# Packed attention with a gated convolution: the same instructions in another written-out order

## The chip, the cores and the metric

The kernel runs on one core of a Trainium2 chip. The metric is the device time of one execution in microseconds (us). Three runs of the kernel before took 290.02, 289.56 and 290.32 us; their median is 290.02 us.

## What is computed

For each of 8 batches, 8 heads of width 64 attend in two stages: 32 learned queries `p` attend to the 576 keys and values, and the 576 queries `q` attend to the 32 packed results. The heads side by side are `x` (576 x 512 a batch), which goes through a causal convolution over 5 positions, a sigmoid gate, a product with `w_val` and a product with `w_out`:

```python
p_packed = sm_attn(p, k, v)             # 32 x 64 per head
x        = sm_attn(q, p_packed, p_packed)
gate_pre += conv_w[k] * xp[:, k:k + S]  # k = 0..4, causal
out      = (sigmoid(gate_pre) * (x @ w_val)) @ w_out
```

`w_val`, `conv_w` and `w_out` reach the kernel as 64-bit floats, so each weight comes as two 32-bit words, and the kernel itself makes two float32 parts of them.

## The kernel before, in words

The work of one batch is cut into **streams**, Python generators that issue a few instructions and yield. The table `streams` (line 656) names them by a letter, and the text `ORDER` (line 50) says which stream takes its next step when: `W0.3` is three steps of stream W, `a2` one step of batch 2's stream a. Instructions stand in the queues of the engines in exactly that order (`InOrder`, line 76, ties each to the one before it on its engine). Nothing is rearranged later, so the text is the schedule, and an instruction whose input is late holds up all that stands behind it on its engine.

Capital letters load or prepare weights. `L` loads the word tiles of `w_val` (wv0 to wv3, 512 KB each), of `conv_w` and of `w_out` (wo0 to wo3). `P`, `K`, `Q`, `V` load p (two batches at once, four transfers of 64 KB) and k, q, v of a batch (two transfers of 576 KB each). All are issued by SyncE (SP) in one queue. `W` turns wv0 to wv3 into the float32 tile `wv`: a tile takes two ScalarE instructions (`top`, `words`), three on VectorE and two on GpSimd (`from_double`, line 232, and line 257). `O` does the same for `w_out` and splits it into a high and a low part, `woh` and `wol`; `C` does it for `conv_w`, turns it on TensorE (`cwps`, `spread`) and leaves `cwb`.

Small letters are the work of a batch:

- `k`, `q`: VectorE transposes p, k, q (`pT`, `kT`, `qT`).
- `a` (`attn_pack`, line 349): scores `s1` on TensorE, their row maximum `nb1` on VectorE, exp on ScalarE (`a1`), a turn on TensorE (`at`), its copy `a1t` on ScalarE, the product with v (`pv`), the scaled copy `ppd`.
- `p`: the turn of `ppd` (`ppTt`) and its copy `ppT`.
- `s`, `t`: scores `s2`, and their softmax by VectorE, GpSimd and ScalarE in `t2`; the result is `a2` with a high part `a2h` and a low part `a2l`.
- `w`: packed values times `wv` (`wp`), split into `wph` and `wpl`.
- `x` (`mixed`): the attention output. In batches 0 to 2 TensorE does the convolution as well (`convolved`, line 508: 80 small matmuls a half, with `kx` = `ppd` times `cwb`); from batch 3 on stream `g` does it on VectorE, 16 instructions a batch.
- `v` (`value`, line 571): 12 long matmuls for each quarter of the columns (`val`), the gated product `sig`, its high part `gvh` (ScalarE) and low part `gvl` (GpSimd).
- `o` (`project`, line 617): the product with `w_out`, 12 long matmuls for each chunk of 128 output rows, its copy `osb`, and the store. Even batches do chunks 0 to 3 of their pair, odd batches 4 to 8. A chunk accumulates in the one PSUM buffer of tag `out` (`PSB`, line 44), so the next chunk's first matmul waits for the `osb` of the chunk before it. For the last batch (line 621) chunks 4 to 8 are accumulated together, three of four column quarters ahead of the last one; there chunk 4 and 5 share one buffer, and chunk 7 has the `out` buffer.

The profiler names an instruction by its tiles without numbers: `s`, `pv`, `x`, `val`, `o` are these matmuls, and all have line 84, that of the helper.

## Time and profile before

| What | Value |
|---|---|
| median of three runs | 290.02 us |
| the profiled execution, its own time | 290.36 us |
| its span in the trace | 288.6 us |
| first matmul | 12.92 us |
| first matmul of `val` (batch 0) | 59.2 us |
| busy: TensorE, VectorE, ScalarE, GpSimd | 257.3, 236.6, 163.7, 127.8 us |
| read from and written to HBM | 33.57 MB, 9.44 MB |

Times inside the trace count from the start of the span; the execution's own time is 1.76 us more than the span. A busy TensorE is not a TensorE at its peak: matmuls overlap, and one that runs at half the clock counts as busy all the same.

### The profile page before, as it was taken

How to read it: one execution, taken by the hardware profiler on the slowest of the kernel's cores; microseconds unless marked ns; L12 is line 12 of the kernel's file. 1: busy time of each engine (PE TensorE's matmuls, PEld its weight loads, DVE VectorE, ACT ScalarE, POOL GpSimd, SP SyncE). 2: the span in 40 equal slices, each digit the busy share in tenths (PEclk: the TensorE clock that was granted, in tenths of full speed). 3: DMA queues.
4: the chain of work that ended last, by engine and by line, in shares of the span. 5: the costliest groups of instructions: out<-in, count | busy, mean ns of one | idle time of the engine just before them, and what ended most of it. 6: DMA issues, size and time to landing. Idle time of an engine off the chain costs nothing.

```text
span 288.6 us, 8496 instructions
## 1 busy us (share of the span) xinstructions
PE 257.3 (89%) x3676; PEld 190.6 (66%) x3676; DVE 236.6 (82%) x313; ACT 163.7 (57%) x306; POOL 127.8 (44%) x118
## 2 busy tenths in 40 slices
PE   0147758998999999999999999999999999999994
PEld 0025446476677867678678778676887688688873
DVE  0599478598989897869999999999999899777811
ACT  2363464457873646666583776566684763754322
POOL 0153668736798972305335631534044534312410
PEclk9999999999999999999999999999999999999999
DMA  6999962649576849451136456421411111111104
GB/s 238 337 354 314 297 228 75 218 131 301 185 216 201 274 111 271 154 156 41 40 125 209 140 194 204 125 75 39 118 39 39 74 39 73 40 73 73 39 0 182
DMA packets 25839, 43.56 MB, mean 151 GB/s; under 512 B 5829, under 2 KB 11973, under 8 KB 25802
## 3 DMA queue, kind: packets, MB, share of 16 engines
q1 hardware_dynamic: 25802, 43.02, 46.3%
q8 instruction: 29, 0.48, 0.7%
q14 instruction: 8, 0.07, 0.1%
HBM read 33.57 MB, written 9.44 MB: 149 GB/s over the span
## 4 chain that ended last, share of the span: by engine, by line
PE 65%; DVE 22%; ACT 5%; DMA 4%; issue 2%; POOL 0%; SPq 0%; ACTq 0%; DVEq 0%
PE o L84 27%; PE val L84 13%; DVE sig L84 10%; PE s L84 7%; PE x L84 7%; PE pv L84 4%; DMA wv_words<-in_moe_w_val_dram 4%; PE wp L84 2%; PE at L84 2%; DVE qT L84 2%; DVE t L84 2%; DVE mx L84 2%; DVE kT L84 1%; ACT sig L84 1%; DVE rs L84 1%
## 5 line engine op out<-in xcount | busy, mean ns | idle before, releaser
L84 POOL TENSOR_TENSOR gvl<-sig,gvh 128x576 fp32r<-128x576 f32 x32 | 49.0, 1533 | 85.5 <-ACT gvh L84 85.5
L84 DVE SCALAR_TENSOR_TENSOR sig<-xp,cw,sig 128x576 f32<-128x576 f32 x80 | 73.4, 917 | 6.1 <-ACT sig L84 4.5
L84 PE MATMUL o<-woh,gvh 128*128 128x512 f32 x144 | 58.6, 407 | 0.7 <-ACT osb L84 0.7
L84 PE MATMUL o<-woh,gvl 128*128 128x512 f32 x144 | 56.8, 395 | 0.0
L84 PE MATMUL o<-wol,gvh 128*128 128x512 f32 x144 | 56.7, 394 | 0.0
L84 PE MATMUL val<-a2h,wph 128*128 128x288 f32 x128 | 39.3, 307 | 0.1
L84 PE MATMUL val<-a2h,wpl 128*128 128x288 f32 x128 | 37.8, 295 | 0.0
L84 PE MATMUL val<-a2l,wph 128*128 128x288 f32 x128 | 37.7, 295 | 0.0
L84 PEld LDWEIGHTS o<-woh,gvh 128*128 128x128 f32 x144 | 27.0, 188 | 11.3 <-ACT osb L84 2.1
L84 ACT ACTIVATE osb<-o 128x512 f32<-128x512 f32 x34 | 20.2, 596 | 22.1 <-PE o L84 18.0
L84 PEld LDWEIGHTS o<-woh,gvl 128*128 128x128 f32 x144 | 27.0, 188 | 6.4
L84 ACT CAST gvh<-sig 128x576 fp32r<-128x576 f32 x32 | 21.5, 671 | 16.6 <-DVE sig L84 16.4
L84 PEld LDWEIGHTS o<-wol,gvh 128*128 128x128 f32 x144 | 27.1, 188 | 5.0
L84 PE MATMUL s<-kT,pT 32*32 32x288 f32 x512 | 17.2, 480 | 14.2 <-DVE kT L84 13.3
L84 DVE SCALAR_TENSOR_TENSOR sig<-sig,val 128x576 f32<-128x576 f32 x32 | 23.7, 740 | 7.5 <-PE val L84 4.5
L84 PEld LDWEIGHTS val<-a2h,wph 128*128 128x128 f32 x128 | 24.0, 188 | 5.7 <-issue 1.3
L84 POOL TENSOR_TENSOR t<-t,rs 128x576 f32<-128x576 f32 x16 | 20.8, 1298 | 14.7 <-DVE rs L84 14.5
L84 PEld LDWEIGHTS val<-a2h,wpl 128*128 128x128 f32 x128 | 24.1, 188 | 0.6
L84 PEld LDWEIGHTS val<-a2l,wph 128*128 128x128 f32 x128 | 24.1, 188 | 0.0
L84 PE MATMUL pv<-vm,a1t 96*32 96x64 f32 x768 | 17.0, 244 | 7.9 <-ACT a1t L84 7.3
L84 PEld LDWEIGHTS pv<-vm,a1t 96*32 96x32 f32 x768 | 13.8, 125 | 15.3 <-ACT a1t L84 9.7
L84 POOL TENSOR_TENSOR t<-t,mx 128x576 f32<-128x576 f32 x16 | 18.5, 1159 | 11.0 <-DVE mx L84 9.9
(80 smaller groups left out, 452.0 us busy)
## 6 DMA issues: line engine op xcount, KB each, us to landing
km<-in_k_dram SPq DMA_DIRECT2D x16, 576.0 KB, 5.9
vm<-in_v_dram SPq DMA_DIRECT2D x16, 576.0 KB, 5.8
qm<-in_q_dram SPq DMA_DIRECT2D x16, 576.0 KB, 6.0
out_dram<-osb SPq DMA_DIRECT2D x36, 256.0 KB, 2.0
wv_words<-in_moe_w_val_dram SPq DMA_DIRECT2D x4, 512.0 KB, 4.4
wo_words<-in_moe_w_out_dram SPq DMA_DIRECT2D x4, 512.0 KB, 5.8
p<-in_p_dram SPq DMA_DIRECT2D x16, 64.0 KB, 5.5
cw_words<-in_moe_conv_w_dram SPq DMA_DIRECT2D x1, 20.0 KB
```

Source lines behind the costliest of these rows:

```text
L84: made = getattr(self.engine, op)(*args, **kw)
```

## The change

Only the text of `ORDER` changes. Every stream takes the same number of steps, so every engine executes the same instructions on the same data; what changes is where they stand. The first line and the last lines of the table:

```diff
-L0 W0 L0.2 P0.2 k0 K0.2 L0 W0 L0 W0.2 L0 k0 K1 W0.2 k0 V0 W0.3 a0 O0 K1 O0 W0.2 Q0 W0.2 a0.3 V0 Q0 W0 O0 k1 W0 C0.2 O0
+L0 K0 W0.3 P0 K0 W0.2 L0 P0 W0.3 k0.3 W0.4 L0 a0 K1 W0.2 V0 W0.4 L0 W0.2 K1 a0.2 W0 a0.3 W0 a0 L0 k1 a0 C0.2 W0 k1
...
-v7 g7 v7 g7 v7 o7.2 g7 v7 o6 o7.2 v7.2 o7.15
+o6 g7 v7.2 g7 o6 g7.2 o6 g7.2 v7 o6 x7 g7.2 v7 g7.2 v7.4 g7 o6.2 g7.3 v7.2 g7.4 v7.3 o7 g7 o7.2 v7.3 o7.2 o6 o7.14
+o6.3
```

**SyncE, start of the program, before** (`wv` are tiles of w_val, `km` halves of k, `vm` of v; the number after the name is the batch, or for `wv` and `wo` the tile):

```order
L84 DMA wv0_words_77<-in_moe_w_val_dram 128x1024
L84 DMA wv1_words_81<-in_moe_w_val_dram 128x1024
L84 DMA wv2_words_83<-in_moe_w_val_dram 128x1024
L84 DMA p_0_85<-in_p_dram 32x8x64 x4
L84 DMA km_0_0_93<-in_k_dram 128x2x576
L84 DMA km_0_1_95<-in_k_dram 128x2x576
L84 DMA wv3_words_97<-in_moe_w_val_dram 128x1024
L84 DMA cw_words_100<-in_moe_conv_w_dram 5x1024
L84 DMA wo0_words_104<-in_moe_w_out_dram 128x1024
L84 DMA km_1_0_108<-in_k_dram 128x2x576
L84 DMA vm_0_0_114<-in_v_dram 96x4x384
```

and in the changed kernel:

```order
L84 DMA wv0_words_77<-in_moe_w_val_dram 128x1024
L84 DMA km_0_0_79<-in_k_dram 128x2x576
L84 DMA p_0_85<-in_p_dram 32x8x64 x4
L84 DMA km_0_1_90<-in_k_dram 128x2x576
L84 DMA wv1_words_94<-in_moe_w_val_dram 128x1024
L84 DMA wv2_words_111<-in_moe_w_val_dram 128x1024
L84 DMA km_1_0_148<-in_k_dram 128x2x576
L84 DMA vm_0_0_152<-in_v_dram 96x4x384
L84 DMA wv3_words_159<-in_moe_w_val_dram 128x1024
L84 DMA km_1_1_163<-in_k_dram 128x2x576
L84 DMA cw_words_193<-in_moe_conv_w_dram 5x1024
```

k of batch 0 now stands ahead of wv1 and wv2, k of batch 1 and v of batch 0 ahead of wv3; the first tile of `w_out` has gone from the ninth entry to behind the first v and q.

**ScalarE, its row behind the first exp, before** (`a1` is the exp, `top` and `words` the two weight instructions of a tile):

```order
L84 ACTIVATE a1_0_0_168,sm1_0_120<-s1_0_0_121,nb1_0_0_166 128x576
L84 ACTIVATE wv2_top_180<-wv2_words_83 128x512
L84 ACTIVATE cw_top_182<-cw_words_100 5x512
L84 ACTIVATE cw_words_100<-cw_words_100 5x512
L84 ACTIVATE a1_0_1_186,sm1_0_120<-s1_0_1_122,nb1_0_1_170 128x576
L84 ACTIVATE wv2_words_83<-wv2_words_83 128x512
L84 COPY a1t_0_0_199<-at_0_0_200 96x768
```

and in the changed kernel:

```order
L84 ACTIVATE a1_0_0_167,sm1_0_113<-s1_0_0_114,nb1_0_0_165 128x576
L84 ACTIVATE a1_0_1_172,sm1_0_113<-s1_0_1_115,nb1_0_1_170 128x576
L84 ACTIVATE wv3_top_176<-wv3_words_159 128x512
L84 COPY a1t_0_0_179<-at_0_0_180 96x768
L84 ACTIVATE cw_top_198<-cw_words_193 5x512
L84 ACTIVATE cw_words_193<-cw_words_193 5x512
L84 ACTIVATE wv3_words_159<-wv3_words_159 128x512
```

Between the first exp and the copy `a1t` four weight instructions stood; one is left, and three have gone behind the copy. On VectorE the three instructions of wv0 now come first of all, and those of wv1 and wv2 stand between `kT` and `nb1` of batch 0.

**TensorE, the first two chunks of batch 5's projection, before** (`o_5_4` is chunk 4, `val_6_0` the first quarter of batch 6's values; the last three of 12 matmuls and the first three of the next 12):

```order
L84 MATMUL o_5_4_3321<-woh_70,gvh_643 128x512
L84 MATMUL o_5_4_3321<-wol_71,gvh_643 128x512
L84 MATMUL o_5_4_3321<-woh_70,gvl_644 128x512
L84 MATMUL val_6_0_3334<-a2h_6_2924,wph_6_3311 128x288
L84 MATMUL val_6_0_3334<-a2h_6_2924,wpl_6_3312 128x288
L84 MATMUL val_6_0_3334<-a2l_6_2925,wph_6_3311 128x288
```

and in the changed kernel:

```order
L84 MATMUL o_5_4_3312<-woh_70,gvh_461 128x512
L84 MATMUL o_5_4_3312<-wol_71,gvh_461 128x512
L84 MATMUL o_5_4_3312<-woh_70,gvl_462 128x512
L84 MATMUL o_5_5_3340<-woh_70,gvh_461 128x512
L84 MATMUL o_5_5_3340<-wol_71,gvh_461 128x512
L84 MATMUL o_5_5_3340<-woh_70,gvl_462 128x512
```

Chunk 5 now follows chunk 4 at once; the 12 matmuls of `val_6_0` that stood between them come behind both. Three other places on TensorE matter below: `wp` of batch 0 stood behind the first half of `x` and now stands ahead of it; between chunks 2 and 3 of batch 4 there stood `x`, 12 matmuls of `val` and `x`, and now one `x` alone; and the 12 matmuls of batch 6's chunk 3 stood ahead of `val_7_3` and are now the last on the engine, behind the last product of batch 7. In all else TensorE's order moves by a place or two.

## The prediction

> **What bounds the kernel now.** The first view is the page's busy line, then the busy time by stage (columns: stretch, its length, busy time and instructions of TensorE, its weight loads, VectorE, ScalarE, GpSimd; granted clock, DMA share, GB/s).

> ```profile
> PE 257.3 (89%) x3676; PEld 190.6 (66%) x3676; DVE 236.6 (82%) x313; ACT 163.7 (57%) x306; POOL 127.8 (44%) x118
> 0.00:12.90 12.90, 0.00 (x0) 0.00 (x0) 2.77 (x5) 4.25 (x6) 0.70 (x6) 1.00 0.86 299
> 12.90:59.20 46.30, 34.42 (x763) 20.83 (x763) 36.30 (x51) 22.75 (x48) 29.20 (x25) 1.00 0.77 240
> 59.20:130.00 70.80, 69.60 (x1343) 51.63 (x1341) 61.31 (x88) 45.30 (x95) 41.02 (x37) 1.00 0.66 202
> 130.00:185.00 55.00, 54.29 (x716) 41.68 (x713) 54.06 (x71) 35.80 (x63) 24.23 (x21) 1.00 0.45 141
> 185.00:281.00 96.00, 95.98 (x851) 74.33 (x849) 80.80 (x101) 53.80 (x92) 32.68 (x29) 1.00 0.15 54
> ```

> From 59.2 to 281 us TensorE is busy in 219.9 of 221.8 us: nothing reordered there can gain much unless work disappears, and none does. VectorE is as full only from 130 to 185 us (54.06 of 55). The time that can be won lies ahead of 59.2 us. How much TensorE has to do there, the chain of waits tells (start, length, what):

> ```profile
> 14.51 2.44 PE s L84 x47
> 22.73 1.51 PE pv L84 x48
> ...
> 32.08 2.57 PE s L84 x63
> ...
> 47.72 5.00 PE x L84 x80
> 52.72 1.19 PE wp L84 x16
> ...
> 59.22 1.80 PE val L84 x12
> ...
> 79.76 2.66 PE x L84 x80
> ...
> 89.52 2.78 PE o L84 x12
> ...
> 211.66 0.81 PE pv L84 x48
> ...
> 217.37 1.54 PE s L84 x63
> ...
> 269.77 11.22 PE o L84 x48
> ```

> The same 48 `pv` take 1.51 us early and 0.81 late, `s` 2.57 and 1.54, 80 `x` 5.00 and 2.66: until after 47.7 us the array runs at about half speed, though the stage rows put the granted clock at 1.00. So the first 59 us hold 12.9 us without a matmul and then small, slow matmuls between waits; from there on the program is a dense row of long matmuls (0.234 us each for `o`, 11.22/48). If that row starts earlier by some us and stays dense, the end comes earlier by as much.

> **The start, step by step.** These rows of the timeline carry it (start, length, engine, operation; in brackets the idle time before it and who ended it):

> ```profile
> 0.74 1.32 SPq L84 DMA_DIRECT2D wv_words<-in_moe_w_val_dram  x3
> ...
> 9.43 0.63 ACT L84 ACTIVATE p<-p 128x512 f32<-128x512 f32 x1 [4.78 <-DMA p<-in_p_dram]
> 10.09 0.45 DVE L84 STREAM_TRANSPOSE pT<-p 128x256 f32<-128x256 f32 x1 [10.09 <-ACT p L84]
> 12.79 0.39 DVE L84 TENSOR_SCALAR wv_words<-wv_top 128x512 uint32<-128x512 uint32 x1
> 13.09 1.37 DVE L84 STREAM_TRANSPOSE kT<-km 128x1152 f32<-128x1152 f32 x1
> 16.98 1.42 DVE L84 TENSOR_REDUCE nb<-s 128x1 f32<-128x576 f32 x2
> 17.77 0.74 ACT L84 ACTIVATE a<-s,nb 128x576 f32<-128x576 f32 x1 [1.88 <-DVE nb L84]
> 20.09 0.65 ACT L84 ACTIVATE cw_words<-cw_words 5x512 f32<-5x512 uint32 x1
> 21.90 0.77 ACT L84 COPY a1t<-at 96x768 f32<-96x768 f32 x1
> 22.73 1.51 PE L84 MATMUL pv<-vm,a1t 96*32 96x64 f32 x48 [3.08 <-ACT a1t L84]
> 34.67 0.79 DVE L84 STREAM_TRANSPOSE t<-s 128x576 f32<-128x576 f32 x1 [3.62 <-PE s L84]
> 45.57 0.78 DVE L84 STREAM_TRANSPOSE a<-t 128x576 f32<-128x576 f32 x1 [1.04 <-POOL t L84]
> 45.50 1.54 POOL L84 TENSOR_TENSOR kx<-ppd,cwb 128x640 f32<-128x640 f32 x1
> ```

> and these of the windows (last column GB/s) and of the tile `wv_words` (ns, minimum, median, maximum):

> ```profile
> 0.00:10.00 10.00, 0.00 (x0) 0.00 (x0) 0.00 (x0) 2.51 (x4) 0.70 (x6) 1.00 0.80 263
> 10.00:20.00 10.00, 4.57 (x76) 1.85 (x76) 9.77 (x13) 4.88 (x10) 4.87 (x4) 1.00 0.96 342
> L84 DVE SCALAR_TENSOR_TENSOR wv_top<-wv_top,wv_words x4: 629/1054/1674, 10.9 to 43.9; 128x512 uint32<-128x512 uint32 x4
> ```

> *Loads.* SP's first entries move 3 tiles of w_val (0.524 MB each), p (0.262) and k (1.180) before k is whole: 3.01 MB. Now it is one tile, p and k: 1.97 MB, two tiles less, worth 3.1 to 4.0 us at 342 or 263 GB/s. 1.97 MB at 263 GB/s is in by 7.5 us; p, in front of k's second half, between 5.2 and 7.5. I take 7.3, since p lands late now (9.43). Then p's scaling 0.63, `pT` 0.45, two `kT` of 1.37, hand-overs 0.2: `kT` whole at 11.3 instead of 14.46 (13.09+1.37). **3.1 us earlier**; at least 1 if the small rows of p stay the slow part.

> *To the first `pv`.* Behind `kT` VectorE now has six weight instructions ahead of `nb`: for wv1 and wv2 two of 0.39 and one SCALAR_TENSOR_TENSOR each. That one took from 0.63 to 1.67 us, the long one beside GpSimd work. With wv1 at 0.63 and wv2 at 1.67 the six end at 11.3+3.9=15.2, `nb` (2 x 0.71) at 15.9 and 16.6, the second exp at 17.6 (0.74+0.19 for its sum). On ScalarE one weight instruction (0.66) stands ahead of `a1t`: copy done at 19.0, `pv` at 19.1 against 22.73. **3.6 earlier**: the three weight instructions put behind the copy give back what the six on VectorE take. [...]

> *To the scores of q.* VectorE goes on at 17.6 with the sums (0.3), `pT`, two `kT`: 21.1. Scores of batch 1 21.2 to 23.8, `pv` 25.3; `ppd`, one exp in between, 1.5; `ppTt` 0.9, `ppT` 0.5: `s2` of batch 0 at 28.4 against 32.08. The q transposes (two of 1.37 behind `nb` at 25.4) end at 28.2, so they do not hold it. **3.6 earlier**; v and q stand in the load queue earlier than they are used.

> *To `x` and `val`.* From the end of `s2` to the last `a2` there are now 34.67 to 46.35 us, 11.7. The new chain has the same links, with `kx` and the low part of the first half ahead of the second half's product on GpSimd: about the same, `a2` whole at 31.0+11.7=42.7. Before, `x` then waited to 47.72 for `kx` (45.50+1.54) and a `ppTt`; now `kx` lies earlier, and `x` starts at 42.9, **4.8 earlier**. From `x` to `val` there were 11.5 us; `wp` (1.19) has left that stretch for the wait ahead of it, and `ppTt` (0.5, half speed) has come in, with waits of a few tenths for PSUM: 11.0, so `val` at 53.9 instead of 59.22, 5.3 earlier. A dozen hand-overs in this sum are priced at their old values; I take **5.0**, with ends at 1.5 (the loads bring 1.0 and only half a us is won later) and 6.5.

> The weights lose nothing that is needed: `wv` is whole before `wp` asks; the first `w_out` tile is late by some 15 us, but `o` first asks at 89.52 us. That slack covers it; without it each us late would be a us on the end.

> **The dense part and the end.**

> ```profile
> 280.58 0.40 PE L84 MATMUL o<-woh,gvl 128*128 128x512 f32 x1
> 281.01 0.60 ACT L84 ACTIVATE osb<-o 128x512 f32<-128x512 f32 x1 [4.25 <-PE o L84]
> 281.66 0.50 PE L84 MATMUL o<-woh,gvh 128*128 128x512 f32 x1 [0.69 <-ACT osb L84]
> 282.73 0.69 DVE L84 TENSOR_SCALAR osb<-o 128x512 f32<-128x512 f32 x1 [6.68 <-PE o L84]
> 276.90 1.43 POOL L84 TENSOR_TENSOR gvl<-sig,gvh 128x576 fp32r<-128x576 f32 x1 [4.68 <-ACT gvh L84]
> PE x L84 <- DVE a L84: 0.5, 1, 0.5
> ```

> The price of a matmul that waits for the copy of the one before it is there: 1.08 us from start to start (280.58 to 281.66) instead of 0.23, so **0.85**. Chunk 5 of batch 5 right behind chunk 4 pays all of it. Chunk 3 of batch 4 behind one `x` (some 0.7 us) pays 0.2. Together 1.05; nothing if TensorE would have waited anyway, 2.5 if ScalarE is held up ahead of these copies. In return `a2` of batch 5, for which `x` waited 0.5, now stands further ahead of it: -0.5. Other moves are two places or less and count as nothing: VectorE's order has the gated products and `a2` on average earlier against TensorE's than before.

> At the end the 12 matmuls of batch 6's chunk 3 (2.8 us) stand last. The sum of TensorE's work is the same, but two waits arise: the chunk needs chunk 7's buffer, whose copy by VectorE takes 0.69 plus 0.15 for the hand-over and is covered by chunk 8's three matmuls (3 x 0.234) only: +0.2. And the last quarter is asked for 2.8 us sooner after `val_7_2`, while its `gvl` (276.90+1.43=278.33) was ready 2.25 us ahead of the matmul that takes it (280.58): 2.8 less 2.25 is 0.5, of which ScalarE gives some back, since it no longer copies chunk 3 (0.60) in between: +0.3. Together **+0.5**; at most 2.8, if the last chain does not move at all.

> Sum against the profiled execution: -5.0 -0.5 +1.05 +0.5 = -3.95, 290.36 to 286.4. The median of the runs is 0.34 under that execution, so the median after comes to **286.1 us**.

> **Rivals.**

> *The clock comes earlier (faster).* The rows of `x` show the half speed kept through 80 matmuls from 47.72 on, 5.00 us, and gone by 79.76. If full speed is reached before `x`, that `x` takes 2.66: 2.3 us more, 283.8; with the start's upper end 282.7. For it: the work from `spread` to `pv` stands closer together now, `wp` included. Against: gaps of 0.6 to 2 us ahead of `x` remain, as before. [...]

> *The start's gain does not arrive (no change).* p may land no earlier than k's second half, and ScalarE or VectorE may be held up by wv1 and wv2, which now land later than they are queued for. With 1.5 won at the start, -1.5 -0.5 +1.05 +0.5 is -0.45: 289.6.

> *VectorE sets the end (slower).* It is busy 54.06 of 55 us from 130 to 185. If its queue, and not TensorE, sets the pace from there on, the last `gvl` stays at 278.33, and 27 matmuls come behind it instead of 15. TensorE then ends at 278.33 + 25 x 0.234 + 0.85 + 0.3 = 285.3 where it ended at 284.7, and the 1.05 of chunk waits delay VectorE's own inputs: +1.7, 291.7. It decides if VectorE cannot begin batch 3's gate sooner. Against it: VectorE has 9.5 us free between 59.2 and 130 (70.80-61.31), and that gate starts from an `x` of TensorE's row.

> **How the numbers follow.** The forecast has 0.70, the clock rival 0.10, no change 0.09, slower 0.11. The forecast's own range is 283.2 (start 6.5, waits half) to 289.0 (start at 2.1). The range for all, 282.7 to 289.6, takes in the clock rival and the edge of no change and leaves out slower and a little at each end. A measurement of this kernel tells about 0.3% (0.87 us) from no change: faster is below 289.15. Faster 0.80, same 0.09, slower 0.11.

> **What would show it.** In the changed kernel's trace: first matmul near 9.9 us, first `pv` near 19, `s2` of batch 0 near 28.4, `x` near 43, first `val` near 54, each within 1.5 us; the first `o` by about as much earlier as `val`; a wait of 0.7 of `o` for `osb` twice, in batch 5 and at the end; the last matmul near 281. It is wrong if the first `val` comes after 57.5, or if that gain is there and TensorE's row behind it has new waits of more than 2.5 us in sum.

## The result, and the profile after

| Kernel | Median | Runs | Ratio to before, 95% interval |
|---|---|---|---|
| before | 290.01 us | 8 (289.07 to 291.42) | |
| changed | 287.76 us | 8 (286.24 to 288.72) | 0.9916 (0.9888 to 0.9944) |
| changed, a second time (e9 below) | 287.10 us | 11 (285.75 to 289.43) | 0.9911 (0.9880 to 0.9943) |

The change is a gain of 2.25 us, where 3.95 was forecast. Over all 19 runs the median is 287.24, a gain of 2.8. The profiled execution shown here took 288.72 us, the longest of the first eight (span 286.9); the one profiled later took 287.10 (span 285.3). All fences of this section are of this first execution. Executions over 1.5% above the fastest of their kernel on a chip (two of e5's, one each of e8's and e12's, three of before's) are left out of the medians and ratios below.

The busy line of the page and the same five stretches as before (columns as there):

```profile
PE 257.1 (90%) x3676; PEld 191.0 (67%) x3676; DVE 236.1 (82%) x313; ACT 164.6 (57%) x306; POOL 132.3 (46%) x118
0.00:12.90 12.90, 3.56 (x64) 1.14 (x64) 6.73 (x11) 5.68 (x8) 3.66 (x9) 1.00 0.84 295
12.90:59.20 46.30, 32.82 (x802) 21.36 (x799) 37.97 (x55) 25.02 (x53) 27.42 (x25) 0.82 0.84 246
59.20:130.00 70.80, 69.92 (x1325) 52.83 (x1325) 59.01 (x80) 44.33 (x92) 41.07 (x37) 0.98 0.68 199
130.00:185.00 55.00, 55.00 (x662) 43.07 (x658) 51.98 (x71) 35.35 (x64) 24.16 (x20) 1.00 0.44 135
185.00:281.00 96.00, 93.60 (x834) 71.20 (x833) 80.40 (x99) 53.60 (x90) 36.02 (x29) 1.00 0.18 63
```

TensorE now works in the first stretch (3.56 us), and the second holds 39 matmuls more in less busy time. The 0.82 there is not a slower clock than before: the record of the granted clock begins at 53.07 us in the trace of before and at 22.12 us here, and what lies ahead of it is printed as 1.00, though 63 `s` took 2.57 us there in before, and 1.54 later. The last stretch, where TensorE was busy for 95.98 of 96 us, now has 2.4 us of gaps. One of them, 0.69 us, was there before too, but at 281.66, outside the stretch; the rest gives back a part of the gain.

The start (timeline; start, length, in brackets the idle time before and who ended it):

```profile
6.87 0.63 ACT L84 ACTIVATE p<-p 128x512 f32<-128x512 f32 x1 [1.61 <-DMA p<-in_p_dram]
7.90 2.59 DVE L84 STREAM_TRANSPOSE kT<-km 128x1152 f32<-128x1152 f32 x2
13.94 1.39 DVE L84 TENSOR_SCALAR wv_words<-wv_top 128x512 uint32<-128x512 uint32 x1
15.25 1.41 DVE L84 TENSOR_REDUCE nb<-s 128x1 f32<-128x576 f32 x2
18.87 1.51 PE L84 MATMUL pv<-vm,a1t 96*32 96x64 f32 x48 [0.97 <-ACT a1t L84]
25.69 1.07 PE L84 MATMUL pv<-vm,a1t 96*32 96x64 f32 x27 [2.03 <-issue]
29.68 2.59 PE L84 MATMUL s<-qT,ppT 32*32 32x288 f32 x64 [0.57 <-ACT ppT L84]
35.28 1.70 PE L84 MATMUL spread<-cw_top,ident 5*32 5x64 f32 x51 [1.52 <-issue]
43.59 3.47 PE L84 MATMUL x<-a,kx 32*64 32x288 f32 x80
52.86 0.40 PE L84 MATMUL val<-a2h,wph 128*128 128x288 f32 x1
57.13 0.31 PE L84 MATMUL pv<-vm,a1t 96*32 96x64 f32 x5
59.13 1.04 PE L84 MATMUL pv<-vm,a1t 96*32 96x64 f32 x43 [1.69 <-issue]
```

`kT` is whole at 10.49 (it was 14.46), the first `pv` comes at 18.87 (22.73), the first `val` at 52.86 (59.2): 6.3 us earlier. New is the word "issue": in three rows of small matmuls TensorE stops in the middle of a group that waits for no data, for 2.03, 1.52 and 1.69 us. The third costs more than its length, as the clock column of two windows shows (the third number from the end of the row):

```profile
43.60:47.00 3.40, 3.28 (x86) 1.84 (x81) 3.40 (x5) 1.96 (x5) 2.77 (x3) 1.00 0.09 21
60.10:63.20 3.10, 3.10 (x13) 2.90 (x12) 0.40 (x1) 1.15 (x3) 1.31 (x2) 0.52 0.55 134
```

and the chain of waits (start, length, what):

```profile
57.44 1.69 issue
59.13 1.04 PE pv L84 x43
60.17 3.12 PE val L84 x12
64.04 1.78 PE val L84 x12
```

`x` already runs at full granted clock (80 matmuls in 3.47 us; it was 5.00, and 2.66 in later rows), but right behind the third gap the clock is halved, and the 12 `val` from 60.17 take 3.12 us where those from 64.04 take 1.78. The rows of TensorE from 185 us on that begin with a wait, and the last copy:

```profile
227.70 0.50 PE L84 MATMUL o<-woh,gvh 128*128 128x512 f32 x1 [0.69 <-ACT osb L84]
237.20 0.51 PE L84 MATMUL o<-woh,gvh 128*128 128x512 f32 x1 [0.27 <-ACT osb L84]
264.56 0.50 PE L84 MATMUL o<-woh,gvh 128*128 128x512 f32 x1 [0.59 <-DVE sig L84]
276.97 0.50 PE L84 MATMUL o<-woh,gvh 128*128 128x512 f32 x1 [0.69 <-ACT osb L84]
283.25 0.60 ACT L84 ACTIVATE osb<-o 128x512 f32<-128x512 f32 x1 [2.58 <-PE o L84]
```

The first is chunk 5 behind chunk 4 of batch 5, as forecast; the third, at the first product of batch 7, waits for a `val` buffer that `sig` still reads, and was not forecast. The fourth is the one that stood at 281.66.

### The profile page after: what moved, and what is told of

Same layout as the page of the kernel before. It is cut to its first block, busy times and chain, and to the rows that moved or that the text cites. A ratio compares the mean times of both kernels' runs of the same rounds, so it can differ in the third digit from the quotient of the medians.

```text
span 286.9 us, 8501 instructions
## 1 busy us (share of the span) xinstructions
PE 257.1 (90%) x3676; PEld 191.0 (67%) x3676; DVE 236.1 (82%) x313; ACT 164.6 (57%) x306; POOL 132.3 (46%) x118
## 4 chain that ended last, share of the span: by engine, by line
PE 66%; DVE 18%; ACT 6%; issue 4%; DMA 2%; POOL 1%; SPq 1%; ACTq 0%; DVEq 0%
PE o L84 26%; PE val L84 13%; DVE sig L84 10%; PE s L84 8%; PE x L84 7%; PE pv L84 5%; PE at L84 4%; DMA wv_words<-in_moe_w_val_dram 2%; PE wp L84 2%; ACT sig L84 1%; PE ppTt L84 1%; ACT a L84 1%; SPq L84 1%; PE spread L84 1%; DVE a2l L84 1%
## 5 line engine op out<-in xcount | busy, mean ns | idle before, releaser
L84 POOL TENSOR_TENSOR gvl<-sig,gvh 128x576 fp32r<-128x576 f32 x32 | 51.3, 1604 | 64.7 <-ACT gvh L84 64.5
L84 DVE SCALAR_TENSOR_TENSOR sig<-xp,cw,sig 128x576 f32<-128x576 f32 x80 | 71.1, 888 | 3.2 <-ACT sig L84 1.8
L84 PE MATMUL o<-woh,gvh 128*128 128x512 f32 x144 | 58.9, 409 | 2.3 <-ACT osb L84 1.6
L84 PE MATMUL o<-woh,gvl 128*128 128x512 f32 x144 | 56.9, 395 | 0.0
L84 PE MATMUL o<-wol,gvh 128*128 128x512 f32 x144 | 56.7, 394 | 0.0
L84 PE MATMUL val<-a2h,wph 128*128 128x288 f32 x128 | 39.9, 312 | 0.0
L84 PE MATMUL val<-a2h,wpl 128*128 128x288 f32 x128 | 38.5, 301 | 0.0
L84 PE MATMUL val<-a2l,wph 128*128 128x288 f32 x128 | 38.2, 299 | 0.0
L84 PEld LDWEIGHTS o<-woh,gvh 128*128 128x128 f32 x144 | 27.0, 188 | 13.7 <-ACT osb L84 3.6
L84 ACT CAST gvh<-sig 128x576 fp32r<-128x576 f32 x32 | 21.6, 674 | 25.3 <-DVE sig L84 25.2
L84 DVE SCALAR_TENSOR_TENSOR sig<-sig,val 128x576 f32<-128x576 f32 x32 | 23.7, 740 | 10.5 <-PE val L84 7.0
L84 PEld LDWEIGHTS o<-woh,gvl 128*128 128x128 f32 x144 | 27.1, 188 | 6.8 <-POOL gvl L84 0.5
L84 ACT ACTIVATE osb<-o 128x512 f32<-128x512 f32 x34 | 20.3, 596 | 17.8 <-PE o L84 14.8
L84 PEld LDWEIGHTS o<-wol,gvh 128*128 128x128 f32 x144 | 27.1, 188 | 5.0
L84 POOL TENSOR_TENSOR t<-t,mx 128x576 f32<-128x576 f32 x16 | 20.1, 1254 | 21.8 <-DVE mx L84 21.8
L84 POOL TENSOR_TENSOR t<-t,rs 128x576 f32<-128x576 f32 x16 | 21.9, 1368 | 17.4 <-DVE rs L84 17.3
L84 PEld LDWEIGHTS val<-a2h,wph 128*128 128x128 f32 x128 | 24.6, 192 | 5.2 <-issue 2.0
L84 PEld LDWEIGHTS val<-a2h,wpl 128*128 128x128 f32 x128 | 24.6, 192 | 0.8 <-DVE wpl L84 0.3
L84 PEld LDWEIGHTS val<-a2l,wph 128*128 128x128 f32 x128 | 24.6, 192 | 0.0
L84 ACT ACTIVATE sig<-sig 128x576 f32<-128x576 f32 x20 | 13.7, 685 | 19.0 <-DVE sig L84 18.9
L84 PE MATMUL s<-kT,pT 32*32 32x288 f32 x512 | 16.0, 461 | 9.5 <-DVE kT L84 9.3
L84 PEld LDWEIGHTS pv<-vm,a1t 96*32 96x32 f32 x768 | 13.3, 119 | 13.9 <-issue 6.1
```

The source lines that it names most:

```text
L84: made = getattr(self.engine, op)(*args, **kw)
```

## The experiments

**The start and the rest apart (e1, e2, e9, e10).** e1 has the changed order up to the first `val` of batch 0, and from there the steps that are left, in the order of before. e2 is the other way round.

The seam of e1, against the changed order (what is left of each stream follows as it stands in before):

```diff
 O0.3 q1 a2 O0 x0 p1 a2.2 k3 V2 L0 v0
-v0 a2.2 K3 v0 a2 O0 K3 a2 s1 x1 a2 k3 O0 s1 a2
+K3 O0 K3 a2 v0 k3 a2.2 k3 s1 a2 s1 x1 v0 a2 s1
...
```

Expected of e1: 

> The changed order up to the first val of batch 0, from there on the order of before. Theory (the gain is made ahead of the first val; a part is lost again by a gap of TensorE inside pv of batch 2, where it waits for no data, by the half clock behind it, and later by the chunk waits of batch 5 and by VectorE): the first val starts near 53 us as in the changed kernel, the same at, s2, pv of batch 2 follow it, so the gap is there again and only the chunk wait and the new end are gone: 286.5 us (285.8 to 287.3). Rival (VectorE's row sets the pace from batch 3 on, whatever comes ahead of it): 289 us or more. Rival (the new order of the rest is itself a gain): over 288.3 us.

Expected of e2: 

> The order of before up to the first val of batch 0, the changed order from there on. Theory: the first val starts near 59 us and the rest costs its own waits: -0.5 for x of batch 5, +1.05 for the chunk waits, up to +0.5 at the end, so 290.5 to 291.1 us. Rival (the rest is a gain by itself, the start is not what counts): 288.5 us or less.

Measured: e1 285.32 us (6 runs; ratio 0.985, 0.982 to 0.9879), e2 292.29 us (12 runs; 1.0068, 1.0042 to 1.0094). Later both halves stood on one chip:

Expected of e9, the changed kernel again: 

> The changed kernel itself a second time, beside the next three on one chip. Theory (the gap in pv_2_0 is there in each execution, since the fetch of instructions meets the same loads; the drop to half clock behind it only where the clock's windows of 3.4 us happen to lie so that one of them holds most of the gap): gap of 1.4 to 1.9 us ahead of the 43 last pv again, half clock at 60 us perhaps; 287.0 to 288.5 us. Rival (the gap was a chance of one execution): no gap.

Expected of e10, e1 again: 

> e1 a second time (the changed order up to the first val, the order of before behind it), on the same chip as the changed kernel. Theory (the rest of the changed order costs 2 us more than that of before): 1.5 to 3 us under the changed kernel. Rival (e1 was better by its chip alone): within 1 us of the changed kernel.

e9 took 287.10 us, e10 286.15 us (0.9893, 0.9863 to 0.9924). Together e1 has 285.83 over 12 runs, 1.4 us under the changed kernel's 287.24 over 19, and 4.2 under 290.0. So the start alone is worth 4.2 us, and the changed rest costs: 1.4 behind the new start, 2.3 behind the old one. Against what was expected, e1 is a little too fast (0.5 under its range by the median of all 12) and e2 too slow by 1.2. The distance of e9 and e10 on one chip, 0.95 us, meets the rival's "within 1 us", and their intervals overlap. So by medians alone the cost of the rest is clear of noise only behind the old start (e2); behind the new one it rests on the pooled runs and on the traces.

Where the rest loses is read from the traces, at points where TensorE has done the same work in both. The table gives how much later the kernel with the changed rest starts a group than e1 (e3, explained below, is the changed kernel without the third gap; the second pair is e9 and e10; in the third, both have the old start):

```
                         e3 - e1    e9 - e10    e2 - before
first val                  +0.2       +1.3        -0.7
o of batch 2, chunk 3      -0.6       +0.8        -1.4
wp of batch 6 (222 us)     -2.1       -0.7        -2.8
o of batch 6 (246 us)      -0.1       +1.3        -0.8
end of the last matmul     +1.3       +2.7        +0.7
```

From line to line, all three pairs agree: from the first `val` to `wp` the changed middle gains about 2.2 us (-2.3, -2.0 and -2.1), the stretch of the chunks from 222 to 246 us loses 2.0 in each, the end loses 1.4, 1.5 and 1.5. In sum +1.1, +1.4 and +1.4, near the 1.4 of the pooled medians.

**The gaps of TensorE (e3, e6).** A third gap, 1.69 us in the middle of `pv_2_0`, where nothing is waited for: my theory was its supply of instructions. The view of the transfers of the changed kernel, for 51.7 to 56.4 us and for 56.4 to 57.8, has of the queue q8 in the first nothing and in the second one packet:

```profile
DMA packets 794, 1.52 MB, mean 324 GB/s; under 512 B 32, under 2 KB 335, under 8 KB 794
q1 hardware_dynamic: 794, 1.52, 103.5%
...
DMA packets 724, 0.29 MB, mean 207 GB/s; under 512 B 645, under 2 KB 723, under 8 KB 723
q1 hardware_dynamic: 723, 0.27, 112.6%
q8 instruction: 1, 0.02, 5.6%
```

The page counts 29 such packets of 16 KB in the whole run, against 3676 matmuls and as many weight loads: one for each 127 pairs (`q8 instruction: 29, 0.48, 0.7%`, the second number in MB). The three gaps lie behind the matmuls number 221, 348 (127 later) and 855 (four times 126.8 later), and wherever a trace with this start has a gap in these rows, it is behind one of these numbers. So in these rows a gap stands where one packet's instructions end and the next has not come. What the trace has for the block that begins with number 856 (us; "need" is my reckoning, the first matmul of the block before):

```
            need    fetch begins  landed  first matmul of it  loads meanwhile
changed     51.70   56.50         57.75   59.13               296 GB/s
e3          51.83   55.53         56.72   58.03               264
e6          51.33   54.60         55.73   57.12               346
before      57.99   58.79         59.77   63.61                73
```

Two edits test it. e3 puts 12 long matmuls where the small ones were:

```diff
-a2 s1 x1 a2 k3 O0 s1 a2 v0.2 s1.3
+a2 s1 x1 k3 O0 s1 v0.2 a2.2 s1.3
```

Expected: 

> The changed order with one pair exchanged: the 12 long matmuls of val_0_1 stand ahead of the 48 small ones of pv_2_0 instead of behind them. Theory (TensorE's next 16 KB of instructions are fetched while it runs the last some 20 matmuls of the old ones; small matmuls use those up before the fetch has landed, long ones do not): the fetch near 56.5 us now lies under val, the gap of 1.7 us inside pv_2_0 goes or falls under 0.4, and without it the clock does not drop near 60 us, so val_0_1 takes 1.6 us instead of 3.1: 2 to 3 us earlier at 65 us, and 285.0 to 286.5 us at the end. Rival (the gap is a wait for data or for a buffer that the profile does not name, bound to pv_2_0): the gap stays ahead of or inside pv_2_0, 287.8 us. Rival (VectorE sets the pace later): gap gone, but 287.3 us or more at the end.

e3: no gap at this place, although the fetch was late again (55.53). Two things made up for the 1.69 us: the fetch landed 1.0 us earlier than in the changed kernel (56.72 for 57.75), and the five matmuls ahead of number 856 were `val` and took 0.76 us (57.27 to 58.03), where five `pv` had taken 0.31.

```profile
57.27 0.40 PE L84 MATMUL val<-a2h,wph 128*128 128x288 f32 x1
59.05 0.88 PE L84 MATMUL pv<-vm,a1t 96*32 96x64 f32 x48
59.86 0.82 PE L84 MATMUL at<-ident,a 64*96 64x64 f32 x12
```

The clock did not drop either, `at_2_1` comes 3.4 us earlier than in the changed kernel (59.86 for 63.22), and 2.75 of it stay to the end of the trace (span 284.2 for 286.9). But the median, 287.64 us (6 runs; 0.9924, 0.9896 to 0.9951), is that of the changed kernel, above the 285.0 to 286.5 expected, and as high as the rival with VectorE had it. The profiled execution of e3 (285.96) was its fastest, that of the changed kernel (288.72) its slowest.

How much the gap differs from one execution to the next, the other traces show. e10 and e1 are the same kernel, with `pv_2_0` as in the changed one; e1 has no gap there and e10 has one. e7, explained below, has the exchange of e3 and a gap all the same:

```profile
58.16 0.86 PE L84 MATMUL pv<-vm,a1t 96*32 96x64 f32 x43 [1.16 <-issue]
58.58 0.29 PE L84 MATMUL val<-a2l,wph 128*128 128x288 f32 x1 [0.97 <-issue]
```

Each row begins with matmul number 856, of e10 the first and of e7 the second; in e7 it lies in the middle of `val`. That puts the rival "a wait bound to `pv_2_0`" out: the gap stands at a number and behind a fetch, whatever the matmul is. With the long matmuls the gap is 0, 0 and 0.97 us (e3, e8, e7); without them, in the changed order, 1.69, 1.65, 0.78 and 0.58 (the changed kernel, e4, e9, e5), and only the first of these is followed by half clock. So the first profile had caught a bad case. By the lengths of the five matmuls the exchange is worth 0.45 us here (0.76 less 0.31); the medians do not show it.

e6 takes away a load: p of batches 4 and 5, four transfers in pieces of 256 bytes that were on their way from 54.8 us, goes behind the v of batch 3.

```diff
-v0 t1 a3 a2 P4 v0.2
+v0 t1 a3 a2 v0.2
...
-w1 p2 P4 O0 V3 w1 v0
+w1 p2 O0 V3 P4 w1 v0
...
-v1 x1.2 Q2 k4 q2
+v1 x1.2 Q2 P4 k4 q2
```

Expected: 

> The changed order with the load of p for batches 4 and 5 (four transfers of 64 KB in short pieces, issued at 54.8 us) behind the two v loads of batch 3, its scaling on ScalarE just ahead of its use. Theory (each 127 matmuls TensorE needs 16 KB of new instructions, whose fetch queues behind the loads in flight: 4.8 us from the need to the start of the fetch at 56.5 us, against 0.3 to 1 us where the loads pause): that fetch starts within 3.7 us of its need, the gap in pv_2_0 falls from 1.7 to 0.5 us or less, and the end comes 0.5 to 2.5 us earlier than in the changed kernel: 285.5 to 287.3 us. Rival (the gap belongs to pv_2_0 and has nothing to do with the loads): 1.7 us as before, 287.8 us.

The gap in `pv_2_0` is gone and the fetch began 3.3 us after its need instead of 4.8, as expected. One trace cannot show that the moved load did it: e1, which moves no load, has no gap either and a fetch 3.1 us after its need, and e9 has 4.0. At 66.3 us TensorE was 3.4 us ahead of the changed kernel. Then these rows took back 1.9 us of it, the rest went in smaller pieces (timeline of e6):

```profile
80.30 0.30 PE L84 MATMUL val<-a2h,wph 128*128 128x288 f32 x1 [1.10 <-issue]
83.30 0.40 PE L84 MATMUL val<-a2h,wph 128*128 128x288 f32 x1 [0.51 <-DVE sig L84]
87.72 0.51 PE L84 MATMUL o<-wol,gvh 128*128 128x512 f32 x1 [0.24 <-POOL wol L84]
```

The fetch ahead of the first of these rows began at 78.0 us, 3.8 after its need; in the changed kernel it was 1.2. It was not the moved load that lay in its way: in the view of the transfers from 74.2 us on, no load runs until 75.3, and then those of q and k. Why the fetch had not begun by then, or whether it had been asked for, is open. From 93 us on the two traces differ by less than 0.2 us. The median was 290.20 us (12 runs; 0.9991, 0.9959 to 1.0024): no gain. That it is 3.1 over e9 on another chip, though the profiled span is the 286.9 of the changed kernel's first, I cannot explain in full; the profiled execution was e6's fastest and the changed kernel's slowest of the first eight. No run of the changed kernel is on record for the chip of e5 to e8, so what these four say of it rests on their traces more than on their medians.

**Single moves undone (e4, e5, e8, e7).** e4 puts `val_6_0` back between chunk 4 and 5 of batch 5.

```diff
-s7 g6 o5.2 t7 o5 v6 g6
+s7 g6 v6 o5.2 t7 o5 g6
```

Expected: 

> The changed order with val_6_0 put back between chunk 4 and chunk 5 of batch 5. Theory A (TensorE sets the pace there): the 0.69 us wait of o for osb near 227 us is gone, 0.85 us earlier, 286.9 us. Theory B (VectorE is the bound from 223 to 264 us, as the chain of waits of the changed kernel has it): within 0.3 us of 287.8 us.

Measured 291.65 us (12 runs; 1.0058, 1.0031 to 1.0085): slower than the changed kernel by 3.9, and both theories fall. The wait of 0.69 is gone, and a longer one is there (timeline of e4):

```profile
222.97 1.43 POOL L84 TENSOR_TENSOR gvl<-sig,gvh 128x576 fp32r<-128x576 f32 x1 [2.90 <-ACT gvh L84]
222.95 3.69 DVE L84 SCALAR_TENSOR_TENSOR sig<-xp,cw,sig 128x576 f32<-128x576 f32 x2
224.35 1.68 POOL L84 TENSOR_TENSOR t<-t,rs 128x576 f32<-128x576 f32 x1
227.23 0.80 DVE L84 SCALAR_TENSOR_TENSOR sig<-xp,cw,sig 128x576 f32<-128x576 f32 x1
227.95 1.21 DVE L84 TENSOR_TENSOR wpl<-wp,wph 128x1024 fp32r<-128x1024 f32 x1
229.22 0.61 PE L84 MATMUL val<-a2h,wpl 128*128 128x288 f32 x1 [3.69 <-DVE wpl L84]
```

`val_6_0` needs `wpl`, and in the changed order that stands behind the gates on VectorE: it ends at 229.2, when TensorE was ready at 225.5. The clock is halved as well, from 229.05 us for 3.41 us. Two gate instructions beside two GpSimd ones take 3.69 us together, where one that begins ahead of GpSimd's takes 0.80. Chunk 5 behind chunk 4 is thus no blunder: it pays 0.85 to cover 3.7. That `wpl` stands late on VectorE is what lies behind it; no run moved `wpl` itself.

e5 puts chunk 3 of batch 6 back ahead of `val_7_3`, e8 does that on top of e3.

```diff
-g7 v7.2 g7.4 v7.3 o7 g7 o7.2 v7.3 o7.2 o6 o7.14 o6.3
+g7 v7.2 g7.4 v7.2 o6.3 v7 o7 g7 o7.2 v7.3 o7.2 o6 o7.14
```

Expected of e5: 

> The changed order with batch 6's chunk 3 (12 matmuls, its copy and store) put back ahead of val_7_3. Theory A (the new end costs what the traces of the changed kernel and of e1 differ by from o_6_0 on, 0.7 for the wait of o for the buffer of val that sig still reads, 0.3 for gvl, 0.25 for chunk 7's buffer, 1.3 in all): 286.4 us, and the 0.59 us wait of o for sig near 264 us is gone. Theory B (my forecast of 0.5): 287.2 us. Rival (the last gvl sets the end in either order): within 0.3 us of 287.8.

Expected of e8: 

> e3 (val_0_1 ahead of pv_2_0) and e5 (chunk 3 of batch 6 ahead of val_7_3) together. Theory: the prices of the two places add up, 286.3 us (e3 less 1.3). Rival (the end waits for the last gvl): as e3, 287.6 us.

Measured: e5 291.16 us (10 runs; 1.0034, 0.9990 to 1.0079), e8 291.12 us (11 runs; 1.0032, 0.9997 to 1.0066). None of the theories foresaw it. The timeline of e5 has (e8 has the same wait of 3.4 us):

```profile
262.08 0.67 ACT L84 CAST gvh<-sig 128x576 fp32r<-128x576 f32 x1 [2.46 <-DVE sig L84]
262.66 0.59 ACT L84 ACTIVATE osb<-o 128x512 f32<-128x512 f32 x1
263.30 0.80 PE L84 MATMUL o<-woh,gvh 128*128 128x512 f32 x1 [3.43 <-ACT osb L84]
```

Chunk 3 needs the buffer of chunk 2, whose copy stands on ScalarE behind a `gvh` that waits 2.46 us for VectorE. In the changed order TensorE does `val_7_3` and the products of batch 7 meanwhile. Again the moved instruction covers a wait that the order of the other engines makes; and behind the wait the clock is halved for 3.41 us, as in e4 (from 263.27 us in e5, 262.54 in e8).

e7 keeps the changed order (with the swap of e3) up to chunk 7 of batch 3 and takes the order of before for what is left. Its seam:

```diff
 x5 o3 v4 s6.2 t5 v4 q7 a7 t6 o3 v4 s6 a7 g5
-o3 g5 Q7 v4 a7 t6 a7 s6 t6 g5 a7 v4 o3 a7.2
+Q7 g5.2 w5 g5.2 v4 g5 w5 g5 a7.3 o3.3 w5 V7
...
```

Expected: 

> The changed order up to chunk 7 of batch 3, with val_0_1 ahead of pv_2_0 as in e3; from chunk 8 of batch 3 on the order of before (its chunks of batches 4 and 5 and its end). Theory (what the changed rest costs lies behind 190 us: 1.7 us of chunk waits from 223 to 246 us and 1.3 us at the end): 3 us under e3, 284.6 us, and faster than e1 as well. Rival (wpl of batch 6 comes late on VectorE whatever the rest, as in e4): a wait of val for wpl of 2 us or more, 287 us.

Measured 291.52 us (12 runs; 1.0040, 1.0008 to 1.0072). At the seam the first `val` of batch 5 waits for `a2`:

```profile
202.25 0.61 PE L84 MATMUL val<-a2h,wph 128*128 128x288 f32 x1 [4.72 <-ACT a L84]
```

The clock is halved around it, from 200.39 us for 6.83. Neither the 284.6 of the theory nor the wait for `wpl` of its rival came. A seam in another place was not tried. That the changed middle with the old end would beat e1 stays open.

**The start further (e11, e12).** In the profile after, `nb` (15.25) waits for the weight instructions of wv2, though the scores are done at 13.0. e11 is e1 with those behind the row maxima.

```diff
-K1 W0.2 V0 W0.4 L0 W0.2 K1 a0.2 W0 a0.3 W0 a0
+K1 W0.2 V0 W0.2 L0 K1 a0.3 W0.5 a0.2 W0 a0
```

Expected: 

> e1 with VectorE's three instructions on wv2 (and GpSimd's two) behind the two row maxima of batch 0, which waited for them until 15.4 us though the scores were done at 13.1. Theory A (the start is a chain through VectorE): nb at 13.2, first pv at 16.8 instead of 19.0, and 1.5 to 2.2 us of it arrive at the first val: 283.3 us. Theory B (instructions come no sooner than the loads ahead of them): the gap in the middle of pv_0_1 grows from 1.5 us to 2.5 us or more, since the fetch still starts at 22 to 23 us, and the first val comes at most 1 us earlier: 284.5 us or more.

Measured 286.00 us (6 runs; 0.9892, 0.9860 to 0.9924), as e10 beside it. The maxima do come at 13.15 and the turn `at` at 14.92 (17.00 in the changed kernel), but the first `pv` at 18.88:

```profile
17.47 0.67 ACT L84 ACTIVATE wv_top<-wv_words 128x512 f32<-128x512 f32 x1 [1.98 <-DMA wv_words<-in_moe_w_val_dram]
18.05 0.78 ACT L84 COPY a1t<-at 96x768 f32<-96x768 f32 x1
18.88 1.51 PE L84 MATMUL pv<-vm,a1t 96*32 96x64 f32 x48 [3.14 <-ACT a1t L84]
25.70 0.64 PE L84 MATMUL pv<-vm,a1t 96*32 96x64 f32 x27 [1.69 <-issue]
```

The instruction on wv3 that stands ahead of the copy on ScalarE waits for its load. 2.1 us won on VectorE are lost on the next engine, and theory A falls; B is not tested by it, since the matmuls ahead of the gap are no earlier (its time fits, its longer gap did not come).

e12 is e11 with the load of wo0 behind p of batches 2 and 3 and the first v of batch 1, its two ScalarE instructions later.

```diff
-a0 L0 a1 p0 C0 p0 s0 O0.2 W0 a1 s0.6 P2 t0 P2 V1 C0
+a0 a1 p0 C0 p0 s0 W0 a1 s0.6 P2 t0 P2 V1 L0 O0.2 C0
```

Expected: 

> e11 with the load of wo0 behind p of batches 2 and 3 and the first v of batch 1, its two ScalarE instructions behind the second exp of batch 1. Theory B: 0.52 MB less stands ahead of the fetch, which starts 1 to 1.5 us earlier than in e11, the gap in pv_0_1 shrinks by as much, and the first val and the end come 0.5 to 1.5 us before e11. Theory A: no difference from e11 at the first pv, and less than 0.3 us at the first val.

Measured 285.84 us (5 runs; 0.9880, 0.9843 to 0.9916). The fetch ahead of the first gap began at 23.27, in e11 at 23.08, and the gap did not shrink: theory B in the form "it waits behind every byte queued before it" falls. The loads beside it were about as dense, though (312 GB/s from 18.9 to 23.2 us, 326 in e11), since later ones moved up: that it waits for a lull is not tested. What sets the start of a fetch beside loads is open.

## Why the prediction was right, and where it was off

- **Direction and cause: right.** The gain is the start's (e1), and TensorE's row behind it carries it to the end. The loads did what was worked out: `kT` whole at 10.5 (forecast 11.3), the first `pv` at 18.87 (19.1), `x` at 43.6 (42.9), the first `val` at 52.9 (53.9). That the six weight instructions ended at 15.3 (15.2) is luck: they began 0.8 us earlier than forecast, behind the earlier `kT`, and took 4.8 us instead of 3.9. What was long was the last on wv2, a TENSOR_SCALAR of 1.39 us counted at 0.39; the SCALAR_TENSOR_TENSOR of wv1 took 0.69 (counted at 0.63), that of wv2 1.34 (1.67).
- **To the scores of q: off by 1.3 us.** `s2` of batch 0 came at 29.7, not 28.4. The step counted hand-overs between engines and left out that TensorE can stand still for its own instructions; the 2.03 us gap in `pv_0_1` is the miss. The trace of before had such a gap of 0.4 us, which I had passed over.
- **The clock rival (0.10) came about, but not as a gain on top.** In every profile with the new start the clock was full by 42 to 46 us (in the one of before, its record begins at 53.1), and the first `x` took at most 3.5 instead of 5.0 us. From `x` to `val` it was 9.3 us where 11.0 were forecast. The gaps of 2.03 and 1.52 us ahead of `x` took back a part, the third gap and the half clock behind it the rest. That the closer row of work ahead of `x` raised the clock, as the prediction argued for this rival, was its estimate; no run separates it.
- **The start's term, -5.0: a little large.** The profile shows 6.3 at the first `val`, the medians 4.2 at the end. The profiled execution of before had no half clock behind 53 us, that of e1 was its fastest; executions of one kernel differ by 2 us and more, and one trace does not show the middle of them.
- **`x` of batch 5, -0.5: right in kind.** Its wait for `a2` is gone. The rest of the changed middle, which I had counted as nothing, is worth more: the middle gains about 2.2 in all.
- **Chunk waits, 1.05: mis-sized.** The wait of 0.69 is where it was put, but the stretch from 222 to 246 us loses 2.0. The price of a wait was about right: the pair of chunks takes 0.94 us more than in e1. Left out was what follows: 0.4 at the wait of 237.20, and the rest in pieces of 0.25 us and less at `val` and `x`. What the gates that take longer beside GpSimd's instructions have in it (in e4 3.69 us for two, 0.80 for one), no run separates.
- **The end, +0.5: mis-sized.** It measured 1.4 to 1.5. The step looked at chunk 7's buffer and the last `gvl`; it missed that without chunk 3 in between the first product of batch 7 stands right behind `val_7_3` and meets a buffer that `sig` still reads (0.59 at 264.56).
- **"VectorE sets the end" (0.11) did not decide, but has a part in it.** TensorE has no such wait from 93 to 223 us; at 229 (`wpl`) and 262 (`gvh` for `sig`) VectorE is what the order of TensorE has to work around.

In sum the rest was forecast at -0.5 + 1.05 + 0.5 = +1.05 and measured +1.1 to +1.4 in the traces. That is luck: each of the three terms was about half of what was measured, or less, and the errors cancel. The start gave 0.8 less. That makes 2.8 over all runs, and 2.25 in the first comparison. Two sums in the prediction are off: a start of 6.5 with half the waits gives about 284, not 283.2, and the clock rival with that start 282.3, not 282.7. The result lies far from both.

## What to carry to other kernels

When an order written out by hand is changed, price it in halves that each hold together (a start with the old rest, the old start with the new rest); a single move put back is not undone, since the instruction that looks misplaced may be covering another engine's wait. An earlier step pays only as far as the next engine's queue lets it: look at what stands ahead of each hand-over there, loads included. And where rows of small matmuls run while loads are heavy, look for idle time called "issue": long matmuls in that place can hide a part of it (here the gap was 0, 0 and 0.97 us with them, 0.58 to 1.69 in the changed order). And take more than one trace of a kernel before a gap is priced.
